# The first pair's up product made before the mix is known, and amended by a low-rank product

## The chip, the core and the metric

The kernel runs on one core of a Trainium2 chip. The metric is the device time of one execution in microseconds (us). Engines are named as in the profile: PE (TensorE matmul) with PEld (its weight loads), DVE (VectorE), ACT (ScalarE), POOL (GpSimd) and SP (SyncE, which here only issues DMAs).

## What is computed

Two stages follow each other: a gated linear recurrence with complex gates over 4 batches, 8 heads, 768 tokens and a head size of 48, and a mixer whose token mixing has rank 32.

```
# recurrence, per batch and head; S is 48 x 48
new_re = ar * S_re - ai * S_im
new_im = ar * S_im + ai * S_re
S_re, S_im = new_re + outer(k[t], v[t]), new_im
y[t] = q[t] @ S_re                       # gates a normalised to a magnitude of at most 0.999

# mixer, on x = y laid out as (batch, token, 8 * 48 = 384)
h  = x.transpose(0, 2, 1) @ U @ V        # U: 768 x 32, V: 32 x 768
u  = x + h.transpose(0, 2, 1)
ch = maximum(u @ w_ch1, 0) @ w_ch2       # w_ch1: 384 x 1536, w_ch2: 1536 x 384
out = u + ch
```

For one batch `u = x + V^T r` with `r = U^T x` (32 x 384). So `u @ w_ch1 = x @ w_ch1 + V^T (r @ w_ch1)`: the second term is a product of rank 32. The first needs only x of the tokens concerned, the second needs r, and so all 768 tokens of the batch.

## The kernel before, in words

Each batch's 768 tokens are six chunks of 128; there are 24 chunks, 0 to 23. For two chunks at a time (a group) `gates` computes magnitudes and angles, and for each chunk `prep` and `chain` do the recurrence in chunked form. A chunk's result x goes into one of eight buffers `xo` (line 873 copies it there from PSUM).

The mixer works on pairs of chunks; there are twelve pairs, three to a batch. `mixer(m)` for the first pair of a batch starts with `rank` (line 898): r as 24 matmul records over all six chunks, copied to SBUF at line 901. Every pair then has

- `spread` (line 914): V^T r for its two chunks,
- `mixed`: u = x + that (DVE, line 333), three transposes a chunk (line 927) and a copy into `uT` (line 929),
- `up` (line 939): six products, each of two 128-column blocks of w1 with the 256 columns of `uT` (12 records each, since an f32 matmul is recorded twice), followed by a Relu on ACT into `h`,
- the down product: for pair 0 `down` (line 1085), twice six pieces of h with w2; for later pairs `down_two` (line 1128), a form with fewer multiplications,
- `leave`: the result is sent out by POOL (line 1072).

The last six pairs use `up_fewer` (line 997) in place of `up`. `uT` and `h` have one buffer each, and the products `up` and `down` share two PSUM tiles (tag "M").

The weights come as 64-bit floats and are turned to f32 on the chip by `single`: twelve pieces of 768 KB and one for U and V, in the fixed order w1 (six), U and V, w2 (six). SP loads a piece into one of two staging slots (line 478), DVE converts it in six instructions (lines 487 to 497) into one of two further slots, and POOL adds it to its place by a DMA (line 500). The first half of w1's columns are pieces 0 to 2, the second half 3 to 5.

The order of all instructions is worked out on the host by `Plan`. Each piece of work is registered with an engine, a cost, a rank, and what it reads and writes. `Plan.order` lets every engine take the ready piece with the lowest rank (on SP and POOL too), and the kernel issues everything in this order. Ranks come from the table `URGENCY` by kind and number ("w1", "w2", "gates", "angles", "prep", "levels", "rest"; its values look like microseconds and are only compared with each other). Two kinds stand outside it: "small" comes before everything, "mixing" (the products `up` and `down`) after everything. So the mixing fills the gaps that the chunks leave. As long as no "mixing" work has begun, an idle PE is given spare products of the identity with itself (line 1252), whose result nobody reads.

Of the kernel before, what the change touches and what calls it, by code (L numbers as in the profile page):

```python
# [10 lines left out]
FP = mybir.dt.float32  # L11
# [12 lines left out]
BLK = 32  # L24

URGENCY = {
    "w1": {0: -1281.04, 1: -1220.88, 2: -1207.45, 3: 315.61, 4: 369.7, 5: 444.04, 6: 70.95},
    "w2": {0: -1266.56, 2: -21.8, 4: -981.82, 6: -74.99, 8: 354.48, 10: -1170.63, 12: 259.42},
    "gates": {0: 253.11, 1: -1390.93, 2: -0.7, 4: -1280.16, 6: 565.76, 8: -1068.17, 10: -187.84, 12: -54.04, 14: 550.2,
        16: 60.85, 18: -1317.29, 20: 219.78, 22: -1069.82},  # L30
    "angles": {0: -1303.82, 1: -1298.68, 2: -1227.51, 4: 58.46, 6: 57.41, 8: -1315.3, 10: -1053.02, 12: 620.73,
        14: 187.25, 16: -891.55, 18: 148.92, 20: -161.38, 22: -1298.55},
    "prep": {0: -1294.88, 1: 125.6, 2: -26.13, 3: 96.73, 4: 102.92, 5: 146.86, 6: 553.65, 7: 283.9, 8: 120.02,
        9: -991.17, 10: -32.91, 11: 113.94, 12: -202.96, 13: 14.8, 14: 318.58, 15: 357.43, 16: 269.94, 17: 521.08,
        18: 158.53, 19: -163.04, 20: 127.47, 21: 184.1, 22: 205.57, 23: -1204.94},
    "levels": {0: 201.22, 1: 294.56, 2: -15.94, 3: 207.38, 4: -1236.01, 5: 275.3, 6: 572.46, 7: 14.34, 8: -1057.92,
        9: 306.71, 10: 125.53, 11: 133.52, 12: 287.15, 13: 373.35, 14: 82.96, 15: 592.16, 16: 289.79,
        17: -1204.78, 18: -1075.08, 19: 91.86, 20: 733.17, 21: -1309.23, 22: 119.93, 23: -1230.17},
    "rest": {0: 93.55, 1: 47.27, 2: 273.41, 3: 257.67, 4: -1050.04, 5: -1068.08, 6: -1240.77, 7: -1208.87, 8: -1033.73,
        9: -1290.81, 10: 34.85, 11: -1143.56, 12: -162.29, 13: -197.24, 14: -1046.5, 15: 612.4, 16: 244.97,  # L40
        17: -1261.21, 18: 98.64, 19: -1031.75, 20: -1297.46, 21: 239.78, 22: 384.61, 23: 164.23},
}

# [144 lines left out]
def kernel(  # L189
# [76 lines left out]
    def buffer(base, tag, bufs, shape, space=None, padded=None):  # L266

        if tag not in pools:
            pools[tag] = pool(tag, bufs, **({"space": space} if space else {}))
        plan.buffer(base, tag, bufs, space is not None)  # L270
        kw = {"padded_shape": padded} if padded else {}
        makers[base] = lambda: pools[tag].tile(shape, FP, tag=tag, name=base[0], **kw)
# [7 lines left out]
    def get(*base):  # L280
        if base not in T:
            T[base] = makers[base]()
        return T[base]

    def psum(base, tag, shape, padded=None):
        buffer(base, "ps" + tag, 2, shape, PSUM, padded)

    def c_act(n):
        return 0.22 + 0.0008 * n  # L290

    def c_dve(n):
        return 0.15 + 0.00104 * n
# [8 lines left out]
    def PE(*a, **kw):  # L302
        plan.add("PE", *a, late=0.17, **kw)

    def ACT(cost, *a, **kw):
        plan.add("ACT", cost - 0.09, *a, late=0.09, **kw)

    def DVE(cost, *a, **kw):
        plan.add("DVE", cost - 0.09, *a, late=0.09, **kw)
# [22 lines left out]
    def add(o, a, b):  # L332
        nc.vector.tensor_tensor(out=o, in0=a, in1=b, op=OP.add)  # L333
# [60 lines left out]
    GATE = singles.tile([128, 6, GC * DM], FP, name="gate")  # L394
    AREA = {nm: GATE[:, n] for n, nm in enumerate(("x", "y", "n", "z", "ar", "ai"))}
    AREA.update({nm: AREA[nm].rearrange("p (c h d) -> p c h d", h=H, d=D) for nm in ("ar", "ai")})
    sums_w = singles.tile([128, 2, KF // 3 * 128], FP, name="sums")
    TS = []
    for n in range(3):
        TS.append(singles.tile([DQ, GC, H * NTOT], FP, name="T%d" % n))  # L400
# [475 lines left out]

    def mixer(m):
        i0 = m * MC  # L880
        b, c0 = where(i0)
# [4 lines left out]
        def out_of(nm, k, shape, padded):  # L886
            psum((nm, k), "M" if nm in ("up", "down") else "T", shape, padded)
            return nm, k

        if c0 == 0:  # L890
            buffer(r, "r", 1, [128, DM])
            ps = out_of("rank", b, [128, DM], [128, 512])

            def rank():
                for k in range(NCH // MC):
                    for n in range(NP):
                        c = n % MC * (NCH // MC) + k
                        nc.tensor.matmul(out=get(*ps)[n * R:(n + 1) * R], lhsT=U[:, c], rhs=get("xo", b * NCH + c), start=(k == 0),
                                         stop=(k == NCH // MC - 1), tile_position=(0, n * R))
            PE(2.0, R0, rank, [("UV", 0)] + [("xo", b * NCH + c) for c in range(NCH)], [ps], steps=2 * NP * NCH // MC)  # L900
            ACT(c_act(DM), R0, lambda: nc.scalar.copy(out=get(*r), in_=get(*ps)), [ps], [r])
        uT, h = ("uT", m), ("h", m)
        buffer(uT, "uT", 1, [128, KD, N])
        buffer(h, "h", 1, [128, KF, N])

        def spread():

            ps = [out_of("mixed", i0 + cc, [128, DM], [128, 512]) for cc in range(MC)]

            def products():  # L910
                for y in range(2):
                    for cc in range(MC):
                        at, c = slice(cc * MC * R, (cc + 1) * MC * R), c0 + cc
                        nc.tensor.matmul(out=get(*ps[cc])[:, y * DH:(y + 1) * DH], lhsT=V[at, c * CH:(c + 1) * CH],
                                         rhs=get(*r)[at, y * DH:(y + 1) * DH], start=True, stop=True, tile_position=(cc * MC * R, 0))
            PE(0.85, R0, products, [r, ("V", 0), uT + ("kept",)], ps, way=5, steps=8)
            return ps

        def mixed(cc, ps):
            i, c = i0 + cc, c0 + cc  # L920
            u = ("xo", i)
            DVE(c_dve(DM), R0, lambda: add(get(*u), get(*ps), get(*u)), [ps], [u])
            tr = out_of("uTp", i, [128, KD, CH], [128, 4, CH])

            def turn():
                for f in range(KD):
                    nc.tensor.transpose(out=get(*tr)[:, f], in_=get(*u)[:, f * 128:(f + 1) * 128], identity=ident)
            PE(0.35, R0, turn, [u], [tr], steps=KD)
            DVE(c_dve(DM), R0, lambda: nc.vector.tensor_copy(out=get(*uT)[:, :, cc * CH:(cc + 1) * CH], in_=get(*tr)), [tr],
                [uT + (cc,)])  # L930

        def up(ff):
            ps = out_of("up", (m, ff), [128, 2, N], None)
            lo = ff * 128 // WP * WP

            def products():
                for e in range(2):
                    for f in range(KD):
                        nc.tensor.matmul(out=get(*ps)[:, e], lhsT=w1[:, f, (ff + e) * 128:(ff + e + 1) * 128],  # L939
                                         rhs=get(*uT)[:, f], start=(f == 0), stop=(f == KD - 1))  # L940
            PE(2.6, RM, products, [uT] + [("w1", f, lo) for f in range(KD)], [ps], takes=[h], steps=4 * KD)
            ACT(c_act(2 * N), R0, lambda: act(get(*h)[:, ff:ff + 2], get(*ps), AF.Relu), [ps], [h + (ff,)])

# [135 lines left out]
        def down(cc):  # L1079
            i, c = i0 + cc, c0 + cc  # L1080
            ps = out_of("down", i, [128, DM], [128, 512])

            def products(f0):
                for ff in (f0, f0 + 1):
                    nc.tensor.matmul(out=get(*ps), lhsT=get(*h)[:, ff, cc * CH:(cc + 1) * CH], rhs=w2[:, ff],
                                     start=(ff == 0), stop=(ff == KF - 1))
            for f0 in range(0, KF, 2):
                PE(1.29, RM, lambda f0=f0: products(f0), [h + (f0,), ("w2", f0)], [ps], steps=4)
            o = ("xo", i)
            DVE(c_dve(DM), R0, lambda: add(get(*o), get(*ps), get(*o)), [ps], [o])  # L1090
            leave(cc)
# [78 lines left out]

        for cc, ps in enumerate(spread()):
            mixed(cc, ps)
        if m >= FEWER:
            up_fewer()
        else:
            for ff in range(0, KF, 2):
                up(ff)
# [24 lines left out]
    def chunks(g):  # L1202
        both = list(range(*GROUPS[g]))
        for these in [both] if g >= PAIRED else [[i] for i in both]:
            for i in these:
                load_qkv(i)
                prep(i)
            together([chain(i) for i in these])
            for i in these:
                if where(i)[1] == NCH - 1:  # L1210
                    for m in range(i // MC - NCH // MC + 1, i // MC + 1):
                        mixer(m)

    for n, nm in enumerate(AREA):
# [92 lines left out]
```

## Time and profile before

| | us |
|---|---|
| median of three runs (695.6 to 698.66) | 697.34 |
| the profiled execution | 698.57 |
| its span, first to last instruction | 696.8 |
| mean granted TensorE clock, share of full | 0.997 |
| first copy of chunk 1's x from PSUM | 83.5 |
| first rank product (batch 0 complete) | 133.1 |
| first up product of pair 0 / of pair 1 | 140.8 / 183.4 |
| rank products of batches 1, 2, 3 | 301.6, 454.7, 590.4 |

A profile's page gives busy time by engine and by groups of instructions; the stretches give the busy time of each engine between two moments; the views in order of time show single instructions. An engine that is busy need not be doing needed work: the spare products count as busy. A wait in the trace is named by the instruction that ended it.

### The profile page before, as it was taken

The page shows a single profiled execution, that of the slowest core. Times are in us where ns is not written, and L with a number is a line of the kernel's source. Part 1 is how long each engine was busy: PE and PEld are TensorE (multiplying, and loading weights), DVE is VectorE, ACT ScalarE, POOL GpSimd, SP SyncE. Part 2 cuts the span into 40 slices and gives each one's busy share as a digit, 9 for nine tenths or more (in the row PEclk, how much of TensorE's full clock was granted, in tenths as well). Part 3 has the DMA queues.
Part 4 walks back from the last instruction along what each step waited for, and adds up shares of the span by engine and source line. Part 5 has one row for each costly group of instructions (what it writes and reads, how often), then busy time and mean ns, then how long its engine had stood idle before and what let it go on. Part 6 is the DMA issues. An engine that isn't in the chain of part 4 may idle for free.

```text
span 696.8 us, 26972 instructions
## 1 busy us (share of the span) xinstructions
PE 673.7 (97%) x12116; PEld 594.2 (85%) x12116; DVE 538.9 (77%) x877; ACT 416.5 (60%) x776; POOL 51.8 (7%) x92
## 2 busy tenths in 40 slices
PE   8988998999999999999999999999998999999998
PEld 8777777786787888888888888889998898999998
DVE  5899999888998887758598668779886884555734
ACT  7879874968886897958796745434524325031230
POOL 5100000012100010001010100000000000000000
PEclk9999999999999999999999999999999999999999
DMA  8884745699514442432243031222111010000000
GB/s 202 190 187 86 172 99 105 171 222 189 110 36 97 87 92 54 94 70 57 51 89 78 3 86 40 45 43 56 37 36 18 14 41 2 18 7 24 7 18 24
DMA packets 165203, 53.24 MB, mean 76 GB/s; under 512 B 154016, under 2 KB 160352, under 8 KB 165088
## 3 DMA queue, kind: packets, MB, share of 16 engines
q1 hardware_dynamic: 161008, 42.26, 28.0%
q0 software_dynamic: 4080, 9.27, 5.9%
q8 instruction: 95, 1.56, 0.9%
q14 instruction: 20, 0.16, 0.1%
HBM read 33.59 MB, written 4.72 MB: 55 GB/s over the span
## 4 chain that ended last, share of the span: by engine, by line
PE 75%; ACT 10%; DVE 9%; issue 3%; DMA 2%; SPq 0%; DVEq 0%; ACTq 0%
PE down L1128 20%; PE few L997 12%; PE up L939 10%; PE tr L705 6%; PE inner L739 5%; ACT gate L327 4%; PE y L864 3%; PE dk L825 3%; DVE QK L330 2%; PE ks ps L810 2%; PE ph L650 2%; PE es ps L583 2%; PE tot L612 2%; PE y L856 2%; PE spare L1252 1%
## 5 line engine op out<-in xcount | busy, mean ns | idle before, releaser
L330 DVE TENSOR_TENSOR QK<-QK,T 112x1024 f32<-112x1024 f32 x120 | 145.4, 1217 | 7.6 <-PE corners L789 4.0
L939 PE MATMUL up<-uT,w 128*128 128x256 f32 x432 | 98.9, 382 | 0.0
L939 PEld LDWEIGHTS up<-uT,w 128*128 128x128 f32 x432 | 80.5, 190 | 12.3
L1005 ACT COPY h<-few 128x512 f32<-128x512 f32 x36 | 20.6, 586 | 95.0 <-PE few L997 78.2
L708 ACT COPY QK<-tr 112x512 f32<-112x512 f32 x96 | 53.0, 586 | 36.5 <-PE tr L705 36.1
L1128 PE MATMUL down<-w,h 128*128 128x192 f32 x396 | 74.1, 331 | 0.0
L327 ACT ACTIVATE gate<-gate 128x768 f32<-128x768 f32 (+1 forms) x91 | 70.2, 789 | 5.3 <-DMA gate<-in_a_re_dram 2.2
L1128 PEld LDWEIGHTS down<-w,h 128*128 128x128 f32 x396 | 63.7, 190 | 3.2 <-issue 1.1
L739 PEld LDWEIGHTS inner<-QK 112*32 112x32 f32 x4608 | 45.4, 109 | 20.7 <-issue 15.4
L333 DVE TENSOR_TENSOR h<-few,h 128x512 f32<-128x512 f32 x54 | 37.1, 690 | 31.3 <-PE few L997 28.7
L739 PE MATMUL inner<-QK 112*32 112x16 f32 (+1 forms) x4608 | 51.3, 190 | 10.4 <-issue 9.3
L1252 PE MATMUL spare<-ident 128*128 128x128 f32 x406 | 57.8, 289 | 1.7 <-POOL ident masks.py:199 1.5
L330 DVE TENSOR_TENSOR QKC<-qk,cs 128x768 f32<-128x768 f32 x48 | 45.7, 953 | 14.9 <-PE tr L705 13.4
L705 PE MATMUL tr<-ident,QKC 128*112 128x128 f32 x384 | 54.2, 276 | 2.8 <-ACT QK L708 1.1
L1252 PEld LDWEIGHTS spare<-ident 128*128 128x128 f32 x406 | 52.0, 200 | 5.5 <-POOL ident masks.py:199 1.5
L333 DVE TENSOR_TENSOR xo<-down,xo 128x192 f32<-128x192 f32 (+1 forms) x79 | 29.6, 385 | 28.5 <-PE down L1128 28.3
L705 PEld LDWEIGHTS tr<-ident,QKC 128*112 128x112 f32 x384 | 42.1, 133 | 10.9 <-ACT QK L708 3.0
L997 PE MATMUL few<-gate,w 128*128 128x128 f32 x336 | 44.0, 279 | 0.0
L1072 POOL DMA_DIRECT2D out_dram<-xo x32 | 18.8, 586 | 321.0 <-DVE xo L333 289.2
L873 ACT COPY xo<-y 64x192 f32<-64x192 f32 x96 | 30.0, 313 | 18.8 <-PE y L864 17.4
L997 PEld LDWEIGHTS few<-gate,w 128*128 128x128 f32 x336 | 40.6, 194 | 0.5
L1128 PE MATMUL down<-stage 128*128 128x192 f32 x198 | 36.8, 329 | 0.1
(131 smaller groups left out, 1242.6 us busy)
## 6 DMA issues: line engine op xcount, KB each, us to landing
stage<-in_moe_w_ch_dram SPq DMA_DIRECT2D x12, 768.0 KB, 5.8
gate<-in_a_re_dram SPq DMA_DIRECT2D x24, 192.0 KB, 3.5
gate<-in_a_im_dram SPq DMA_DIRECT2D x24, 192.0 KB, 3.7
qk<-in_q_dram SPq DMA_DIRECT2D x24, 192.0 KB, 3.4
qk<-in_k_dram SPq DMA_DIRECT2D x24, 192.0 KB, 4.2
VP<-in_v_dram SPq DMA_DIRECT2D x24, 192.0 KB, 3.4
T<-E SPq DMA_DIRECT2D x48, 96.0 KB, 2.7
w<-stage POOLq DMA_DIRECT2D x12, 384.0 KB, 6.0
```

The costliest lines, as they stand in the source:

```text
L327: return nc.scalar.activation(out=o, in_=i, func=f, **kw)
L330: nc.vector.tensor_tensor(out=o, in0=a, in1=b, op=OP.mult)
L333: nc.vector.tensor_tensor(out=o, in0=a, in1=b, op=OP.add)
L705: nc.tensor.transpose(out=get(*ps)[0:DQ, j], in_=get(*qkc)[:, hh * HH + j].rearrange("p u d -> p (u d)")[:, 0:DQ], identity=ident)
L708: ACT(c_act(HH * CH) - 0.05, R1, lambda u=u, hh=hh, ps=ps: nc.scalar.copy(out=get(*QK)[:, u, hh * HH:(hh + 1) * HH], in_=get(*ps)[0:DQ]), ...
L739: nc.tensor.matmul(out=get(*ps)[js, h], lhsT=k_of(h)[:, js], rhs=part(q_of(h)[:, js], "p"), start=True, stop=True, tile_position=(0, j * BLK))
L825: nc.tensor.matmul(out=get(*dk[r])[x:end, h], lhsT=get(*ks)[at, h, x:end], rhs=get(*VPi)[at, h], start=True, stop=True, tile_position=(r * ...
L873: ACT(c_act(HH * D), RR, lambda r=r, u=u: nc.scalar.copy(out=get(*xi).rearrange("p (a u d) -> p a u d", u=2, d=D)[r * HC:(r + 1) * HC, :, ...
L939: nc.tensor.matmul(out=get(*ps)[:, e], lhsT=w1[:, f, (ff + e) * 128:(ff + e + 1) * 128], rhs=get(*uT)[:, f], start=(f == 0), stop=(f == KD ...
L997: nc.tensor.matmul(out=get(*ps)[:, q], lhsT=w()[:, q * 128:(q + 1) * 128], rhs=v[0](), start=(n == 0 and q == 0), stop=True, skip_group_ch ...
L1128: nc.tensor.matmul(out=get(*to)[:, part], lhsT=x(j), rhs=y[:, j], start=(first and j == 0), stop=(j == KH - 1), skip_group_check=not first)
L1252: nc.tensor.matmul(out=spare[0], lhsT=ident, rhs=ident, start=True, stop=True)
```

## The change

For pair 0 alone, the up product is made as soon as chunks 0 and 1 are done, from x in place of u. Its two chunks are transposed into `uT`, and the six products are made in twelve pieces, all in one PSUM tile, each pair of which ACT copies to `h` without a Relu (`early`). When r is known, `amend` turns it, multiplies it by w1 (three blocks of four times 128 columns, lying below each other in one PSUM tile), and adds `(r w1)^T V` to `h` in three rounds; then a Relu is applied to `h` in place. Pair 0's `mixed` still makes u for the final sum, but has no transposes; pair 0's `down` waits for the whole of `h`. A small matrix `pick`, two identities of 32 below each other, sums the two partial results in which r lies. The table `URGENCY` is new throughout, and has a kind "early".

```diff
 URGENCY = {
-    "w1": {0: -1281.04, 1: -1220.88, 2: -1207.45, 3: 315.61, 4: 369.7, 5: 444.04, 6: 70.95},
-    "w2": {0: -1266.56, 2: -21.8, 4: -981.82, 6: -74.99, 8: 354.48, 10: -1170.63, 12: 259.42},
+    "w1": {0: -109.53, 1: -8.04, 2: 345.14, 3: 723.86, 4: 687.07, 5: 445.03, 6: 10.98},
+    "w2": {0: 76.19, 2: -211.9, 4: 131.04, 6: 421.14, 8: -515.83, 10: -186.39, 12: 1.07},
...
+    "early": {0: 98.86, 2: 63.89, 4: 678.21, 6: -80.97, 8: -124.56, 10: -198.18},
 }
...
+    pick = singles.tile([MC * R, R], FP, name="pick")
+    for n in range(MC):
+        nc.gpsimd.tensor_copy(out=pick[n * R:(n + 1) * R], in_=ident[n * R:(n + 1) * R, n * R:(n + 1) * R])
     sums_w = singles.tile([128, 2, KF // 3 * 128], FP, name="sums")
+    rT = sums_w[:, 0, 0:KD * R].rearrange("p (f r) -> p f r", r=R)
+    RW = sums_w[0:3 * R, 1]
...
+    def early():
...
+            PE(0.35, ("early", 0), turn, [("xo", cc)], [tr], steps=KD)
+            DVE(c_dve(DM), ("early", 0), lambda cc=cc, tr=tr: nc.vector.tensor_copy(
+                out=get(*uT)[:, :, cc * CH:(cc + 1) * CH], in_=get(*tr)), [tr], [uT + (cc,)])
...
+        for ff in range(0, KF, 2):
+            ps = ("up", (0, ff))
+            plan.buffer(ps, "first", 1, True)
+            makers[ps] = first
+            w = [("w1", f, ff * 128 // WP * WP) for f in range(KD)]
+            for e in range(2):
+                PE(1.3, ("early", ff), lambda ff=ff, e=e, ps=ps: product(ff + e, get(*ps)[:, e], get(*uT)), [uT] + w, [ps + (e,)],
+                   takes=[h], steps=2 * KD)
+            ACT(c_act(2 * MC * CH), ("early", ff), lambda ff=ff, ps=ps: nc.scalar.copy(out=get(*h)[:, ff:ff + 2], in_=get(*ps)), [ps],
+                [h + (ff,)])
+
+    def product(j, o, x):
+        for f in range(KD):
+            nc.tensor.matmul(out=o, lhsT=w1[:, f, j * 128:(j + 1) * 128], rhs=x[:, f], start=(f == 0), stop=(f == KD - 1))
+
+    def amend():
...
+        def turn():
+            for f in range(KD):
+                nc.tensor.matmul(out=get(*ps1)[:, f], lhsT=get(*r)[0:MC * R, f * 128:(f + 1) * 128], rhs=pick[0:MC * R], start=True,
+                                 stop=True, tile_position=(0, 0))
+        PE(0.3, R0, turn, [r], [ps1], way=5, steps=2 * KD)
+        DVE(c_dve(KD * R), R0, lambda: nc.vector.tensor_copy(out=rT, in_=get(*ps1)), [ps1], [to])
...
+        def weights():
+            for f in range(KD):
+                for g in range(NR):
+                    nc.tensor.matmul(out=get(*ps2)[g * R:(g + 1) * R], lhsT=rT[:, f], rhs=w1[:, f, g * n:(g + 1) * n], start=(f == 0),
+                                     stop=(f == KD - 1), tile_position=(0, g * R))
+        PE(2.7, R0, weights, [to] + [("w1", f, lo) for f in range(KD) for lo in (0, WP)], [ps2], way=6, steps=2 * KD * NR)
+        DVE(c_dve(n), R0, lambda: nc.vector.tensor_copy(out=RW, in_=get(*ps2)[0:NR * R]), [ps2], [to2])
+
+        for four in (((0, 1), (4, 5)), ((2, 3), (8, 9)), ((6, 7), (10, 11))):
...
+                        nc.tensor.matmul(out=get(*ps)[:, e], lhsT=RW[at, j * 128:(j + 1) * 128], rhs=V[at, 0:MC * CH], start=True,
+                                         stop=True, tile_position=(g * R, 0))
+            parts = [[h + (js[0],)] for js in four]
+            PE(1.0, ("mixing", 0), more, [to2, ("V", 0)] + parts[0] + parts[1], both, way=7, steps=8)
+            for js, ps, names in zip(four, both, parts):
+                o = lambda js=js: get(*h)[:, js[0]:js[1] + 1]
+                DVE(c_dve(2 * MC * CH), R0, lambda o=o, ps=ps: add(o(), get(*ps), o()), [ps], names)
+                ACT(c_act(2 * MC * CH), R0, lambda o=o: act(o(), o(), AF.Relu), [], names)
...
         uT, h = ("uT", m), ("h", m)
-        buffer(uT, "uT", 1, [128, KD, N])
-        buffer(h, "h", 1, [128, KF, N])
+        if m:
+            buffer(uT, "uT", 1, [128, KD, N])
+            buffer(h, "h", 1, [128, KF, N])
...
-            PE(0.85, R0, products, [r, ("V", 0), uT + ("kept",)], ps, way=5, steps=8)
+            PE(0.85, R0, products, [r, ("V", 0)] + ([uT + ("kept",)] if m else []), ps, way=5, steps=8)
...
             DVE(c_dve(DM), R0, lambda: add(get(*u), get(*ps), get(*u)), [ps], [u])
+            if not m:
+                return
...
-                PE(1.29, RM, lambda f0=f0: products(f0), [h + (f0,), ("w2", f0)], [ps], steps=4)
+                PE(1.29, RM, lambda f0=f0: products(f0), [h if m == 0 else h + (f0,), ("w2", f0)], [ps], steps=4)
...
-        if m >= FEWER:
+        if not m:
+            amend()
+        elif m >= FEWER:
             up_fewer()
...
                     for m in range(i // MC - NCH // MC + 1, i // MC + 1):
                         mixer(m)
+                elif i == MC - 1:
+                    early()
```

## The prediction

> **What bounds the kernel now.** I read the totals first, then the busy time of each engine by stage, then where the filler matmuls lie, then each engine in order of time around the join (the moment when all six chunks of the first batch are done and its rank product can run).
>
> ```profile
> PE 673.7 (97%) x12116; PEld 594.2 (85%) x12116; DVE 538.9 (77%) x877; ACT 416.5 (60%) x776; POOL 51.8 (7%) x92
> L939 PE MATMUL up<-uT,w 128*128 128x256 f32 x432 | 98.9, 382 | 0.0
> L1252 PE MATMUL spare<-ident 128*128 128x128 f32 x406 | 57.8, 289 | 1.7 <-POOL ident masks.py:199 1.5 <-issue 0.3
> w<-stage POOLq DMA_DIRECT2D x12, 384.0 KB, 6.0
> ```
>
> PE looks full, but 57.8 us of it is the spare product, which computes nothing. By stage, all engines (busy us; PE, PEld, DVE, ACT, POOL) and then the spare product alone:
>
> ```profile
> 84.00:121.00 37.00, 32.52 (x1030) 27.87 (x1029) 34.91 (x54) 21.89 (x45) 2.57 (x3) 1.00 0.52 104
> 121.00:133.10 12.10, 11.77 (x258) 9.35 (x257) 11.35 (x18) 10.99 (x26) 0.00 (x0) 1.00 0.65 176
> 140.80:158.40 17.60, 17.60 (x81) 14.95 (x80) 14.49 (x22) 11.62 (x19) 3.64 (x4) 1.00 0.85 196
> 158.40:301.60 143.20, 140.81 (x2788) 116.26 (x2787) 121.88 (x176) 119.68 (x214) 11.02 (x15) 1.00 0.46 96
> ```
>
> ```profile
> 84.00:121.00 37.00, 10.30 (x72) 1.00 0.52 104
> 121.00:133.10 12.10, 3.16 (x22) 1.00 0.65 176
> 133.10:140.80 7.70, 3.40 (x23) 1.00 0.76 186
> ```
>
> Before the join DVE is the full engine (94% in each of the first two stretches) and PE has room. From 140.8 on PE is full with real work: chunk products first, and the mixing of the finished batch in every gap. PE, SP and POOL in order of time around the join, then two pieces of the chain of waits that give clean PE paces:
>
> ```profile
> 133.13 2.44 PE L898 MATMUL mixed<-xo,UV 128*32 128x384 f32 x24
> 136.37 0.92 PE L914 MATMUL mixed<-r,V 64*128 64x192 f32 x8
> 140.81 7.94 PE L939 MATMUL up<-uT,w 128*128 128x256 f32 x36
> 149.22 7.93 PE L939 MATMUL up<-uT,w 128*128 128x256 f32 x36
> 178.92 4.04 PE L1085 MATMUL down<-w,h 128*128 128x384 f32 x12
> ```
>
> ```profile
> 119.60 1.47 SPq L478 DMA_DIRECT2D stage<-in_moe_w_ch_dram  x1
> 157.12 0.54 SPq L478 DMA_DIRECT2D stage<-in_moe_w_ch_dram  x1
> ```
>
> ```profile
> 114.91 0.86 POOL L500 DMA_DIRECT2D w<-stage  x1 [9.11 <-DVE stage L497]
> 172.12 0.90 POOL L500 DMA_DIRECT2D w<-stage  x1 [5.08 <-DVE stage L497]
> ```
>
> ```profile
> 252.55 2.59 PE up L939 x12
> 301.65 2.07 PE mixed L898 x24
> ```
>
> The up product of pair 0 is the 72 records from 140.8 to 157.0. The weights stand behind it: the six pieces of w2 are loaded from 119.6 to 157.1, one each 7.5 us, through two staging slots; the last is sent to its place at 172.1 and lands 6.0 us later, at 178.1. Pair 0's down product ends at 182.8, and only then is h free (it has one buffer), so that pair 1's up product, the next filler, can start. How much filler is left when the next rank product starts: after 301.65 five pieces of pair 2's down product still follow, some 4.9 us (0.98 each); after the third rank product at 454.7 ten (9.8 us), after the last at 590.4 fourteen (13.7 us).
>
> [...] here it was 0.997 over the span, and real products in the place of spare ones keep PE as busy, so I charge nothing for the clock.
>
> **The change part by part.** PE pace: 12 records of 256 columns in 2.59 us, 0.843 ns a column.
>
> Out of the full stage: the up product, 6 x 2.59 = 15.5 us, and its six transpose records (L927: 11.5 us for 72, so 1.0). Together 16.5 us.
>
> Into it: (a) r turned: 6 records of 32 columns, bounded by six weight loads of 186 ns below 1.1 us and by a spare-like 0.1 each above zero; 0.6. (b) r times w1: 18 records of 512 columns, three column groups abreast, so 6 x 512 = 3,072 columns; the rank product ran at 2.07 us for 6 x 384, 0.90 ns a column: 2.8 us (7.8 if they ran one after another). (c) the correction: 24 records of 256 columns, two abreast: 3,072 columns at 0.843 are 2.6, and three starts at the 0.2 us that L914's eight records took over their 4 x 192 columns: 3.3 (5.8 if not abreast). Sum 6.7 us. Net 9.8 us of PE less after the join.
>
> Into the front: 16.5 us of PE. Chunk 1's x is copied from PSUM by 84.8, so the room runs from about 84 to 133.1: spare 10.3 + 3.2, and PE idle 4.5 + 0.3, together 18.3 us. It fits, 90% full. The second half needs the last w1 piece (sent 114.9, landed 120.9): three pairs of 2.6 us with an ACT copy (0.59) and its handover, some 3.5 us each, are 10.5 us, in a stretch of 12.1. The price is blocking: an early piece is 1.3 us, two spare records are 0.22. A chunk's product that meets one waits half of it, 0.65 instead of 0.11; early pieces fill 15.5 of 49 us, and the chain has about 35 PE steps there: 35 x 0.32 x 0.54 = 6 us if nothing hides it, 0 where DVE sets the pace. DVE is 94% busy there; I take 2 us. DVE's two uT copies (0.55 each) move forward too, inside those 2 us. ACT gets six copies (3.5 us) in a front where it is 59% busy from 84 to 121: nothing. Two small POOL copies at the start lie ahead of the first sums, before 10.7; the first user on PE is at 16.8: nothing.
>
> After the join, on DVE: six adds of 512 columns (L333's h form, 0.69), rT (0.28) and RW (0.69): 5.1 us. They wait for PE, and behind them in DVE's queue stand w2 conversions and the next gates; DVE was 82% busy from 140.8 to 158.4, so I charge nothing by itself. The six Relus cost 0.63 instead of 0.60. No load is added; every load and its SP and POOL issue can move with the new table. The down product of pair 0 now waits for the whole h: r ready at 136.1, then 0.6 + 0.3 + 2.8 + 0.7 with handovers, three rounds of a 1.1 us product and two adds: about 15 us, so at 151, against 158.3 now.
>
> What is late next: w2. Nothing else can fill PE, because h has one buffer. So the 9.8 us don't come out by themselves; what counts is when pair 0's down product ends. Now it ends 4.7 us after the last landing, with 12 records still to do; with an earlier start only the last piece's two products of 1.29 remain, and 0.8 of handover: 3.4, a gain of 1.3 us. Staging itself can tighten: a slot needs 4.1 us of conversion (4 x 0.56 + 2 x 0.95), 0.9 to send, 6.0 to land: 11.0 for two slots, 5.5 a piece against 7.5, so up to 5 x 2.0 = 10 us. DVE, freed of a PE that it waited on, but with 5.1 us more to do, may give some of it; between 0 and 10 I take 4. The sum: -1.3 - 4 + 2 = -3.3 us. That is less than the 4.9 us of filler left at 301.65, so it carries to the end. The profiled execution was 698.57 us (span 696.8 and 1.8 around it) and becomes 695.3; the median, 1.2 lower at 697.34, becomes 694.0.
>
> **The rivals.**
> The full saving (B): the new order pulls the weights forward by some 12 us and all 9.8 us come out, less the 2 us of blocking: 689.5. For it: the whole table is new, and the staging floor allows 10. Against: 4.9 us of filler left at 301.65 caps the gain unless batch 1's chunks get done sooner as well (then 692.4).
> Weights late, slower (C): staging falls a period behind. Pieces pass the two slots strictly in order, w1, U and V, w2. The new table puts w1's pieces 3 to 5 at 724, 687 and 445 (before 316, 370, 444) and w2's at 76, -212, 131, 421, -516, -186 (before -1267, -22, -982, -75, 354, -1171), so DVE picks most of them later. Every us by which the last landing moves past 178.1 delays pair 1 and finds PE with nothing to do. One period, 7.5 us, less the 1.3: 703.5. It decides from a landing 1.3 us late, and can be measured from 4.8. Against it: DVE had gaps in this stage (3.1 us from 140.8 to 158.4) that take conversions whatever their rank.
> Not early after all: if the second half comes after the join, PE's saving shrinks by 7.8 us; it has the same cause as C and is counted there.
>
> **How the numbers follow.** The forecast (A) 0.42, its own range 690 to 697; B 0.18; C 0.36; others near no change or a little slower 0.04. A measurement of this kernel tells about 0.5%, 3.5 us, from no change. A gives 0.19 faster and 0.23 the same; B 0.17 faster, 0.01 the same; C 0.36 slower; the rest 0.02 and 0.02. So faster 0.36, same 0.26, slower 0.38. The range 685 to 706 leaves out B's lowest 0.03, C's upper 0.12 (two periods late, or blocking at its 6 us on top) and 0.02.
>
> **What would show it.** Spare falls from 57.8 to some 41 us, with L939-like products between 84 and the join; the rank product starts at 135 instead of 133; the correction takes 6 to 7 us of PE; PE shows idle time between the correction and the last w2 landing; pair 1's up product starts at about 179 instead of 183; the end moves by what that start moved. The forecast is wrong if the last w2 piece lands well before 172 or after 180, if the rank product slips by over 6 us, or if later stages, whose order the new table also changes, lose or gain more than this one.

## The result and the profile after

The changed kernel took 702.52 us (median of 16 runs, 697.79 to 707.86), the kernel before 697.31 (16 runs, 693.79 to 700.72): a ratio of 1.0069, 95% interval 1.0047 to 1.009. It is 0.7% slower, where a gain of 3.3 us had been forecast. Ratios and intervals here and below leave out runs over 1.5% above a kernel's fastest, which concerns four of experiment 10's 20 runs. The profiled execution of the changed kernel took 700.51 us, with a span of 698.7.

New line numbers: the rank product is L989, the early up product L921 into "first" (L921 into "up" is the later one), r's turn L933, r times w1 L945, the correction L961, the spare product L1348. Three lines from the page of the changed kernel:

```profile
PE 676.3 (97%) x12102; PEld 590.1 (84%) x12102; DVE 542.6 (78%) x885; ACT 418.6 (60%) x782; POOL 53.6 (8%) x94
L921 PE MATMUL up<-uT,w 128*128 128x256 f32 x360 | 82.2, 381 | 0.0
L1348 PE MATMUL spare<-ident 128*128 128x128 f32 x344 | 48.7, 290 | 1.5 <-POOL ident masks.py:199 1.5
```

Spare fell from 57.8 to 48.7 us; real PE work (PE less spare) rose from 615.9 to 627.6, by 11.7. The correction is 7.5 of that; the early pieces, each started by itself and one of them at a clock of 0.50, are busy for 19.3 us where the up product's two runs of 36 records took 15.9. Next PE in order of time (start, duration, then the line; a bracket is the idle time before it and what ended it):

```profile
114.05 0.38 PE L921 MATMUL first<-uT,w 128*128 128x256 f32 x1
116.23 2.50 PE L921 MATMUL first<-uT,w 128*128 128x256 f32 x5 [1.79 <-issue]
145.40 2.14 PE L989 MATMUL rank<-xo,UV 128*32 128x384 f32 x24
148.53 0.85 PE L933 MATMUL rTp<-pick,r 64*128 64x32 f32 x6
150.40 2.78 PE L945 MATMUL rwp<-w,sums 128*32 128x512 f32 x18
155.05 1.13 PE L961 MATMUL up<-V,sums 32*128 32x256 f32 x8
157.88 1.30 PE L961 MATMUL up<-V,sums 32*128 32x256 f32 x8
160.85 1.46 PE L961 MATMUL up<-V,sums 32*128 32x256 f32 x8
164.25 1.56 PE L1177 MATMUL down<-w,h 128*128 128x384 f32 x4
194.35 5.99 PE L921 MATMUL up<-uT,w 128*128 128x256 f32 x27
```

The join moved from 133.1 to 145.4, 12.3 us later. The landmarks, and the same counted from the join:

| | before, us | after, us | after less before | the same from the join |
|---|---|---|---|---|
| rank product of batch 0 | 133.1 | 145.4 | +12.3 | 0 |
| last w2 piece sent | 172.1 | 182.3 | +10.1 | -2.2 |
| pair 1's up product | 183.4 | 194.4 | +11.0 | -1.3 |
| rank product of batch 1 | 301.6 | 310.4 | +8.8 | -3.5 |
| rank product of batch 2 | 454.7 | 461.2 | +6.5 | -5.8 |
| rank product of batch 3 | 590.4 | 595.2 | +4.8 | -7.5 |
| end of the span | 696.8 | 698.7 | +1.9 | -10.4 |

So the saving after the join is there, 10.4 us by the end. The front gave back 12.3. The stretches of all engines in the changed kernel (from:to, length, busy us of PE, PEld, DVE, ACT and POOL, granted clock, DMA share, GB/s), and then the spare product alone in the first two:

```profile
84.00:121.00 37.00, 32.99 (x804) 26.32 (x803) 33.36 (x50) 26.04 (x50) 1.71 (x2) 0.95 0.53 114
121.00:133.10 12.10, 10.61 (x282) 8.74 (x279) 11.04 (x20) 3.88 (x11) 0.86 (x1) 1.00 0.63 119
```

```profile
84.00:121.00 37.00, 2.51 (x14) 1.90 (x14) 0.95 0.53 114
121.00:133.10 12.10, 0.00 (x0) 0.00 (x0) 1.00 0.63 119
```

Spare fell there from 13.5 to 2.5 us as planned, but PE still idles 5.5 us of the 49.1 (4.8 before) and the clock is no longer 1.00. The chain of waits from 84 us to the join, by line, first of before and then of after:

```profile
by line: ACT gate L327 12.0%; PE inner L739 9.7%; PE tr L705 8.9%; issue 8.0%; PE spare L1252 7.1%; DVE QK L330 7.1%; PE y L864 6.8%; PE dk L825 6.7%; ACT GL L327 3.4%; PE ph L653 3.4%; PE ph L650 3.2%; PE y L856 2.6%; ACT xo L873 2.5%; PE 
```

```profile
by line: PE first L921 22.8%; issue 11.4%; ACT gate L328 10.5%; PE dk L831 6.2%; PE spare L1348 5.8%; PE y L870 5.6%; PE inner L745 4.8%; PE tr L711 3.8%; PE ks ps L816 3.6%; ACT QK L714 3.2%; PE y L862 3.0%; ACT GL L328 2.6%; PE ph L656 2.
```

Of the 61.4 us, 22.8%, 14.0 us, are early products standing on the chain itself, and "issue" (PE waits for nothing that the profile shows) went from 8.0% of 49.1, 3.9 us, to 11.4%, 7.0 us. DVE, in all 6.7 us of the chain before (summed over its pieces in that view), has no piece on it after. The theories for the experiments follow from these rows: the early product is on the chain (work); DVE's extra conversion and the new order make the front late (order); stalls and a falling clock do (clock).

### The profile page after: what moved, and what is told of

It reads as the page before. It is cut to its first block, busy times and chain, and to the rows that moved or that the text cites. A ratio compares the mean times of both kernels' runs of the same rounds, so it can differ in the third digit from the quotient of the medians.

```text
span 698.7 us, 26957 instructions
## 1 busy us (share of the span) xinstructions
PE 676.3 (97%) x12102; PEld 590.1 (84%) x12102; DVE 542.6 (78%) x885; ACT 418.6 (60%) x782; POOL 53.6 (8%) x94
## 3 DMA queue, kind: packets, MB, share of 16 engines
q1 hardware_dynamic: 161008, 42.26, 27.8%
q8 instruction: 95, 1.56, 0.9%
## 4 chain that ended last, share of the span: by engine, by line
PE 74%; ACT 12%; DVE 10%; issue 3%; DMA 1%; DVEq 0%; ACTq 0%
PE down L1220 19%; PE few L1089 12%; PE up L921 8%; PE inner L745 5%; PE tr L711 4%; ACT gate L328 4%; PE dk L831 3%; PE y L870 3%; PE ks ps L816 2%; PE es ps L589 2%; PE first L921 2%; PE y L862 2%; PE ph L656 2%; PE tot L618 2%; PE spare L1348 2%
## 5 line engine op out<-in xcount | busy, mean ns | idle before, releaser
L921 PE MATMUL up<-uT,w 128*128 128x256 f32 x360 | 82.2, 381 | 0.0
L921 PEld LDWEIGHTS up<-uT,w 128*128 128x128 f32 x360 | 67.1, 190 | 9.8
L745 PEld LDWEIGHTS inner<-QK 112*32 112x32 f32 x4608 | 45.0, 110 | 16.2 <-issue 10.1
L1348 PE MATMUL spare<-ident 128*128 128x128 f32 x344 | 48.7, 290 | 1.5 <-POOL ident masks.py:199 1.5
L1348 PEld LDWEIGHTS spare<-ident 128*128 128x128 f32 x344 | 44.2, 202 | 4.3 <-POOL ident masks.py:199 1.5
L328 ACT ACTIVATE h<-h 128x512 f32<-128x512 f32 x42 | 26.2, 629 | 27.3 <-DVE h L334 27.2
```

The source lines that it names most:

```text
L328: return nc.scalar.activation(out=o, in_=i, func=f, **kw)
L745: nc.tensor.matmul(out=get(*ps)[js, h], lhsT=k_of(h)[:, js], rhs=part(q_of(h)[:, js], "p"), start=True, stop=True, tile_position=(0, j * BLK))
L921: nc.tensor.matmul(out=o, lhsT=w1[:, f, j * 128:(j + 1) * 128], rhs=x[:, f], start=(f == 0), stop=(f == KD - 1))
L1348: nc.tensor.matmul(out=spare[0], lhsT=ident, rhs=ident, start=True, stop=True)
```

## The experiments

**1 and 2. A third of the early product; long spare products in the old kernel.**

```
# 1, in the early product; two of the three blocks of the sum over x's 384 columns are left out
- for f in range(KD):  matmul(o, w1[:, f, j], x[:, f], ...)
+ for f in range(1):   matmul(o, w1[:, f, j], x[:, f], ...)
# 2, in the kernel before: 12 of the last 57 spare products, one in four
- matmul(spare, ident, ident)                      # 128 columns
+ for f in range(3): matmul(spare, ident, ident twice side by side)  # 256 columns, 1.3 us
```

> The changed kernel with its order kept, but each early product made of one matmul in place of three, so that 24 records instead of 72 run in the front, 10.3 us of PE less; the two thirds of x @ w1 that are left out are missing in pair 0's h. Theory P (PE's own time and its long pieces hold the chunks up): the first rank product comes at about 137 instead of 145.4, and the end some 8 us earlier. Theory O (the new order of the work on DVE and elsewhere makes the front long, whatever PE carries): the rank product stays at 143 to 146 and the end within 2 us of the changed kernel's.

> The kernel before with its order kept, but 12 of the 57 spare products that lie after 84 us are made as long as an early piece: three matmuls of 256 columns, 1.3 us in place of 0.22, some 13 us more on PE, as much as the change puts there. Nothing else differs. Theory P: the first rank product slips from 133.1 by 6 to 10 us, and the end by about as much. Theory O: it slips by under 3 us, because DVE sets the pace there and PE has 18 us of room.

Experiment 1: 705.39 us, ratio 1.0106 (1.0052 to 1.016). With 10.3 us less PE work the kernel was no faster, and the join came only 1.0 us sooner, at 144.4. The join is theory O's (143 to 146), the end is not: the median lies 2.9 us above the changed kernel's, not clear of noise by the two intervals. One line in order of time and two stretches of it say why neither theory is tested:

```profile
113.94 1.08 PE L831 MATMUL dk<-VP,ks 64*64 64x48 f32 x28 [4.27 <-issue]
```

```profile
110.00:115.00 5.00, 1.06 (x29) 0.97 (x29) 1.43 (x3) 1.61 (x3) 0.00 (x0) 0.68 0.73 204
115.00:120.00 5.00, 5.00 (x134) 3.55 (x137) 3.67 (x7) 1.95 (x4) 0.00 (x0) 0.64 0.07 12
```

PE stood 4.27 us with nothing to wait for in the profile, and ran the next 5 us at a clock of 0.64. The experiment had changed two things, and could not speak on the work.

Experiment 2: 709.04 us, ratio 1.0165 (1.0114 to 1.0216), clock 1.000 in every run. The spare products are now busy for 26.3 us between 84 and the join in place of 13.5. These 12.8 us more of PE work move the old kernel's join from 133.1 to 140.7 and its time by 11.5 us, although the kernel, its order, its weights and DVE's work are the old ones. The join is in theory P's range (6 to 10 us), the end slips by more than P said, and theory O (under 3 us) is out. PE now holds 55.8 of the 56.9 us of the chain from 84 to the join. The room of 18.3 us was not room. Four of the longest stretches of spare products in the old kernel between 84 and the join, in order of time:

```profile
90.57 2.17 PE L1252 MATMUL spare<-ident 128*128 128x128 f32 x18
108.40 1.16 PE L1252 MATMUL spare<-ident 128*128 128x128 f32 x8
115.46 1.83 PE L1252 MATMUL spare<-ident 128*128 128x128 f32 x14
120.74 1.05 PE L1252 MATMUL spare<-ident 128*128 128x128 f32 x7
```

Two of fifteen stretches are longer than one early piece of 1.3 us (the last one shown and its neighbour at 122.05, parted by 0.26 us, would together be a third); the others are 0.4 to 1.2 us. That this shortness is the reason is likely but not shown: no run splits the same work into shorter pieces.

**3 and 4. The stall: the first w2 piece's load later, alone and with a third of the product.** In the changed kernel SP sends U, V and the first w2 piece together at 105.6 to 106.6, and the DMA share is 0.99 from 112 to 114, just before PE's stall of 1.79 us.

```
+ order = plan.order()
+ load = <the SP load of the first w2 piece>
+ order: load moved behind the next six SP loads       # 3: alone; 4: with experiment 1's edit
```

> The changed kernel with one DMA moved in SP's queue: the 768 KB load of the first w2 piece, which is issued at 106.6 right behind U and V and not used before 123, goes behind the next six DMAs, to about 117. Nothing else differs. Theory F ([...] the wait of 1.8 us at 114.4 that nothing in the profile explains, and after it the clock of 0.50 from 116 to 119): the wait shrinks below 0.7 us, the clock stays at 1.0 there, the rank product comes 2 to 4 us earlier than at 145.4 and the end 2 to 3 us earlier. Rival (the wait and the clock are not that load's doing): wait and clock as before, rank product and end within 1 us.

> The same moved load together with the early products cut to one matmul of three (72 records become 24; two thirds of x @ w1 missing in pair 0's h), so that the cut is seen without the 4.3 us wait and the slow clock that covered it. Theory P (PE's time for the early products holds the chunks up): the rank product comes 4 to 8 us before that of the same kernel with whole products, about 136 to 140. Theory O (the order alone makes the front long): within 2 us of it.

Experiment 3: 700.65 us, ratio 1.0049 (1.0027 to 1.0071). Stretches of the changed kernel, then of experiment 3:

```profile
114.00:116.00 2.00, 0.43 (x3) 0.14 (x1) 2.00 (x4) 0.59 (x2) 0.00 (x0) 1.00 0.57 105
116.00:118.00 2.00, 1.77 (x4) 1.50 (x5) 1.31 (x3) 0.00 (x0) 0.00 (x0) 0.50 0.32 56
```

```profile
114.00:116.00 2.00, 2.00 (x72) 1.43 (x72) 1.83 (x4) 0.90 (x3) 0.00 (x0) 1.00 0.54 104
116.00:118.00 2.00, 2.00 (x12) 1.34 (x9) 2.00 (x4) 1.07 (x2) 0.00 (x0) 1.00 0.21 39
```

The stall and the clock of 0.50 are gone from this place, as theory F (both are this load's doing) said. But a clock of 0.50 came elsewhere, from 101.9 to 105.3 after a wait of 1.60 us, so that the mean clock from 84 to 121 stayed at 0.95, and the join came no sooner (146.3). The median is 1.9 us below the changed kernel's; the two intervals overlap, so this gain is not clear of noise.

Experiment 4 (which leaves out what experiment 1 does): 705.95 us, ratio 1.0122 (1.0087 to 1.0156), join at 147.3, within 2 us of experiment 3's, theory O's number. But the stall before the same products as in experiment 1 stayed, 2.35 us in place of 4.27, and the mean clock over its runs was 0.990. With the work taken away PE was busy for 37.2 of the 49.1 us from 84 to 133.1 (43.6 in the changed kernel), and the clock from 84 to 145.4 was 0.93 (0.97); the question of the work stayed open.

What PE waits for in these stalls can be read from the DMA and PE records of the traces. The changed kernel's page has a queue q8 named "instruction", with 95 packets and 1.56 MB. Its packets are 16 KB each, one for each 255 of PE's 24,204 records (matmuls and weight loads). The four waits of the changed front, 1.96, 1.79, 1.49 and 1.32 us long, each end 1.3 to 1.6 us after such a packet has landed. So do the five of the kernel before (0.26 to 1.10 us). From the first of the four waits to the others it is 760, 1,522 and 2,026 PE records, close to 3, 6 and 8 packets' worth; experiment 1's from 100 us on, 0.20, 4.27, 1.19 and 1.32 us, are 253, 253 and 381 matmuls and as many weight loads apart, close to 2, 2 and 3. From these counts I take it that PE was waiting for its own instructions; the profile names nothing that ended the waits. Why a packet comes late isn't shown: the four took 0.88 to 1.11 us themselves, where the median of all is 1.04. In all, such waits grew from 3.4 us in the front before to 6.6 after.

**5. What spare products are worth.**

```
# the kernel before: the last 57 spare products are not issued
- matmul(spare, ident, ident)
+ if len(calls) < 147: matmul(spare, ident, ident)
```

> The kernel before with its order kept, but the last 57 spare products (from 84 us on) left out; they compute nothing. Theory C ([...] the spare products pay): the granted clock falls under 0.99, products in the front show twice their time in places, and the end comes 2 to 6 us later. Rival (spare products only stand in the chunks' way there): the rank product comes 1 to 3 us earlier and so does the end.

702.72 us, ratio 1.0084 (1.005 to 1.0117). Its stretches:

```profile
84.00:121.00 37.00, 27.59 (x891) 22.67 (x892) 33.88 (x52) 20.60 (x43) 2.56 (x3) 0.83 0.51 101
121.00:133.00 12.00, 9.86 (x211) 7.73 (x207) 8.24 (x12) 9.51 (x19) 0.00 (x0) 0.64 0.62 171
```

Without its spare products the front runs at a clock of 0.83 and then 0.64, the join is 6.2 us later and the time 5.4 us longer, as theory C said. So spare products do real service here, and the forecast's "I charge nothing for the clock" was too quick.

**6 and 7. The order.** Each kernel with an order searched for it one instruction at a time, against the planner's own count of the time (a count made before launch, not a measurement: 699.1 to 696.2 for the changed kernel, 697.8 to 694.8 for the one before).

```
- for n in plan.order():
+ for n in ORDER:          # the searched list
```

> The changed kernel with another order and nothing else: each instruction group has its own rank in place of one from the table, searched on the host from the changed kernel's own order by the planner's count (699.1 us for the changed kernel's table, 696.2 for this order; the kernel before's table counts 697.8). Theory T (the new table was not searched well enough, and the structure itself gains): this order is clearly faster than the kernel before, 693 us or less. Theory S (the saved products are given back by the structure, since the correction, the staging of w2 and the longer front cost as much as they bring): it gains the 3 us of the count over the changed kernel and lands at 698 to 700, not below the kernel before by more than 1 us.

> The control: the kernel before with an order searched in the same way, for about as many steps, from its own order (planner's count 694.8 in place of 697.8). Theory S: it gains about 3 us too, to some 694 to 695, and stays 2 to 5 us ahead of the changed kernel with its searched order. Theory T: it gains less than the changed structure, and comes out no faster than that one.

Experiment 6: 702.81 us, ratio 1.0098 (1.0063 to 1.0133), join at 148.2, with a stall of 4.6 us (the profiled execution is the slowest of its six, 706.78). Experiment 7: 699.59 us, ratio 1.0037 (1.0013 to 1.0061), join at 132.3. Neither count came true, nor a theory's time: both searched orders were to gain 3 us, and neither did. Of theory S only the distance came in, 3.2 us between the two kernels (2 to 5). But as the planner's count misled for both, this search says little of what a better order could bring, and the share of the new order in the slip stays open.

**8 and 9. Double the early product; half of it behind the join.** Experiment 2, with 12.8 us more work in the front, had a clock of 1.000 in every run; experiments 1 and 4, with less, had 0.987 to 0.995. So more work should keep the clock out of the answer.

```
# 8: each early piece issued twice, the second over the first
- lambda: product(ff + e, ...)
+ lambda: [product(ff + e, ...) for _ in range(2)]
# 9: pairs 10, 8, 6 of the early product moved behind rank, rTp and rwp
+ for ff, after in ((10, "rank"), (8, "rTp"), (6, "rwp")):
+     <the three instructions of ("early", ff) moved behind that PE step>
```

> The changed kernel with each early product issued twice, the second time over the first: 15.5 us more of PE work before the join, nothing else, and the order kept. P (early PE work lies on the front's path at the rate of the change, 12.3 us of slip for 16.5 us of work, 0.75): the rank product moves from 145.4 to about 157 (152 to 160), and the time to about 712 (708 to 718). O (the slip comes from the new order itself, its conversions and DVE's picks, and PE still has room): the rank product stays under 149 and the time under 706. [...]

> The changed kernel with the second half of the early product (pairs 10, 8 and 6, six of its twelve pieces, 7.8 us, with their copies) moved behind the rank product, in the gaps of the correction's first steps. P (linear, 0.75 us of slip per us of early work): the rank product comes at about 139.5 (138 to 141.5), join to end grows by up to 7.8 us from 553.3, and the time stays where the changed kernel's is, 700 to 703. R (the front has room for half the product, the slip belongs to the second half): the rank product at 136.5 or earlier, and the time 696 to 699. O (the slip is the order's, not the work's): the rank product stays at 143 or later and the time goes to 706 or more.

Experiment 8: 712.69 us, ratio 1.0226 (1.0186 to 1.0265), clock 0.997 to 1.000. The join is at 153.5, 8.1 us later for 15.5 us of added work, and the time 10.2 us longer than the changed kernel's: in theory P's ranges, out of theory O's. Its chain of waits from 84 to 154:

```profile
by line: PE first L921 45.6%; PE inner L745 8.7%; PE ks ps L816 5.3%; issue 4.2%; PE y L870 4.1%; PE tr L711 3.3%; PE spare L1348 3.1%; PE dk L831 3.1%; PE y L862 2.8%; PE es ps L589 2.1%; PE ph L656 1.9%; PE ph L659 1.8%; ACT L325 1.8%; AC
```

45.6% of 70 us are 32 us: practically the whole doubled product (12 x 2.7) stands on the chain. At the join that is 0.52 us per us, close to experiment 2's 7.6 for 12.8 (0.59). It is a net rate: "issue" on the chain fell from 7.0 to 2.9 us here.

Experiment 9: 718.4 us, ratio 1.032 (1.028 to 1.036), the join at 148.3. The numbers are the order theory's, but the run doesn't show its cause, since the clock fell:

```profile
121.00:133.00 12.00, 9.23 (x266) 7.88 (x266) 9.73 (x18) 2.60 (x8) 0.37 (x1) 0.50 0.56 109
146.00:160.00 14.00, 12.35 (x71) 9.09 (x70) 5.72 (x10) 3.68 (x6) 1.62 (x2) 0.87 0.57 128
```

With half the pieces gone from the front it ran at a clock of 0.50 for 12 us, and after the join the moved pieces stand in front of the correction, while DVE is busy 5.72 and ACT 3.68 of 14 us. As a test of the work it is blurred in the way of experiments 1 and 4.

**10 and 11. Shorter pieces, the same number of instructions.**

```
# two of each piece's three matmuls over 16 columns instead of 256; 11: with experiment 3's move too
- matmul(out=o, lhsT=w1[:, f, j], rhs=x[:, f], ...)
+ matmul(out=o[:, :n if f else None], lhsT=w1[:, f, j], rhs=x[:, f, :n if f else None], ...)   # n = 16
```

> The changed kernel with its order and its number of instructions, but of each early product's three matmuls the second and third run over 16 columns instead of 256, so a piece should take some 0.7 us instead of 1.3: about 7 us less PE work before the join and the same count of instructions to fetch. The output leaves out most of two thirds of pair 0's x times w1. W (the slip is the early work itself, at the 0.5 to 0.75 us per us that doubling it and the change show): the rank product moves from 145.4 to 140 to 142, and the time to 696 to 699. K (work taken out of the front only leaves PE idle, and its clock falls): the clock over 100 to 133 drops below 0.9, the rank product stays at 143.5 or later, and the time is 701 or more.

> The same shortened early products, with the first w2 piece's load behind the next six loads, which took away the 1.8 us stall of the changed kernel before. W: no stall over 1 us near 113, clock 1.0 over 108 to 121, the rank product at 139 to 142 and the time 694 to 698. K: a stall of over 1 us appears elsewhere in 100 to 133 with the clock below 0.9 over it, the rank product at 143.5 or later and the time 700 or more.

A piece went from 1.46 us to 0.95, so 6.1 us less work. Experiment 10: 702.01 us, ratio 1.0037 (1.0014 to 1.0061). Experiment 11: 703.16, ratio 1.0092 (1.0057 to 1.0127), join at 147.0, clock 0.78 from 121 to 133. Experiment 10's stretches:

```profile
110.00:121.00 11.00, 9.10 (x281) 7.53 (x280) 9.69 (x14) 6.42 (x15) 0.00 (x0) 0.82 0.61 151
121.00:133.00 12.00, 12.00 (x249) 11.22 (x248) 8.40 (x15) 3.55 (x9) 0.00 (x0) 0.50 0.51 101
```

In the profiled executions the clock theory's numbers came in (0.82 and 0.50, join at 145.9). But experiment 10's runs differ in clock, and so in time, and that helps to tell the two causes apart. Runs at a mean clock of 1.000:

| | runs at clock 1.000 | their median, us | median of all runs |
|---|---|---|---|
| before | 29 of 86 | 695.9 | 697.6 |
| changed | 2 of 16 | 699.6 | 702.5 |
| 3, load moved | 4 of 14 | 698.0 | 700.7 |
| 8, early product doubled | 2 of 4 | 712.2 | 712.7 |
| 10, pieces shortened | 1 of 20 | 695.1 | 702.0 |
| 2, before with long spares | 4 of 4 | 709.0 | 709.0 |

(The 86 are all runs of the kernel before beside the experiments.) At full clock the time grows with the work in the front, but the rates differ: 6.1 us less early work in experiment 10 is worth 4.5 us (699.6 to 695.1, two runs against one), or 0.74 us per us; straight lines of time against clock through all runs of both kernels give 3.2 us at full clock, 0.52. The 15.5 us more of experiment 8 cost 12.6 (0.81), and the 12.8 us more of experiment 2 cost 13.1 (1.02). These are rates of the whole time and hold effects after the join too, so they can't be set against the 10.4 us saved there. At full clock the changed kernel is 3.7 us slower. The rest of the 4.9 us between the medians of the table, 1.2, is clock: the changed kernel's runs have a mean of 0.9961, those of before 0.9978, and their medians lie 2.9 and 1.7 us above their own full-clock values.

## Why the prediction was wrong

**The front, the step that failed.** "The price is blocking: … 6 us if nothing hides it, 0 where DVE sets the pace … I take 2 us." Measured: 12.3 us, against 10.4 saved behind the join. Both ends were too low, for two reasons. First, "room" was counted as a sum (18.3 us of spare and idle PE); experiment 2 shows that 12.8 us put into it are not free, and that its stretches are mostly shorter than a piece (two of fifteen are longer) is the likely reason. Second, DVE's 94% was read as "DVE sets the pace". The chain of waits of before already said otherwise: of its 49.1 us PE holds 27.8, ACT 10.9 and DVE 6.7. A full engine beside a chain isn't the chain. The forecast's half-a-piece estimate, 0.65 us a meeting, supposes that pieces meet the chain at random; in fact nine of the twelve early pieces stood on it whole, 14.0 us of them in the profiled front.

How the 12.3 us divide is not fully shown. PE's waits for instructions, as I read them, which the forecast didn't have, hold 3.1 us more of the chain than before ("issue", 3.9 to 7.0). The 3.4 us at a clock of 0.50 can cost up to half their length, 1.7 us, by my estimate. That leaves some 7.5, about the 7.6 that experiment 2's 12.8 us of work cost in the old order; but this is an estimate from these rows, and what the new order itself brings wasn't separated.

**The clock.** "Real products in the place of spare ones keep PE as busy." PE's busy sum did stay (43.6 against 44.3 us of 49.1), but longer waits replaced short ones (1.3 to 2.0 us in place of 0.3 to 1.1). After the one of 1.79 us the granted clock was 0.50 from 116.0 to 119.4; in the 3.4 us before that spell, as long as the spell itself, PE had been busy for 1.65. This term, charged at nothing, is about 1.2 us of the difference between the medians (2.9 less 1.7).

**The full stage.** Net 9.8 us less PE after the join was forecast. The correction's parts took 0.85, 2.78 and 1.13 + 1.30 + 1.46, so 7.5 us against 6.7: the turn and the correction's rounds were dearer than their terms, r times w1 as computed. Both products ran abreast as priced (2.78 us against 7.8 and 3.9 against 5.8 for one after another). The span from the join to the end fell by 10.4: PE's busy time in it by 7.9 (553.6 to 545.7), less than the net 9.8, and its idle time by 2.5. The forecast let only 5.3 of it come out (3.3 and the 2 of blocking); here it was too cautious. Nearly half of the 10.4 (4.6) comes after batch 2's rank product. Whether the smaller PE load or the new order of the later stages brings that late part wasn't separated; doubling the early product lengthened this span to 559.3, so it also feels the front.

**w2.** "What is late next: w2" came true, and the tighter staging did not. The first piece of w2 before, then the first and the last after:

```profile
134.30 0.86 POOL L500 DMA_DIRECT2D w<-stage  x1 [18.54 <-DVE stage L497]
```

```profile
136.25 0.86 POOL L506 DMA_DIRECT2D w<-stage  x1 [4.45 <-DVE stage L503]
182.26 0.86 POOL L506 DMA_DIRECT2D w<-stage  x1 [6.69 <-DVE stage L503]
```

The first piece was 2.0 us later than before, the last 10.1. The five steps between them took 46.0 us in place of 37.8, so 9.2 a piece in place of 7.6: staging fell about one period behind, as rival C said. The late front doesn't explain that. In experiment 2, with the front 7.6 us late in the old order, the five steps took 38.6 us; in experiments 3 and 8, with the new table, 46.3 and 46.2. The forecast's own sign, "after 180", called it wrong, and pair 1's up product started at 194.4 instead of 179 (counted from the join 1.3 us sooner, where 1.3 plus 4 had been forecast). C's price, a PE with nothing to do, isn't seen: from 164.2 to 194.4 PE was busy 28.96 of 30.2 us, with chunks. What the slower staging costs was not tested by a run of its own. C's number, 703.5, lies close to the measured 702.5, but it has no slip of the front by 12.3 us in it, so that closeness is in part luck.

**The signs.** Spare 48.7 instead of 41 (2.7 us of it run between 133.1 and the later join, another 2.8 between the correction's steps); rank product at 145.4 instead of 135, past the 6 us that were named as the limit; correction 7.5, just over "6 to 7". A small misreading: by its own line pair 0's up product before ended at 157.2, not 157.0; nothing rests on it.

No version here beats the kernel before. The best complete version of the changed kernel is experiment 3, 0.5% slower than before.

## What to carry to other kernels

The sum of idle and filler time on an engine is not yet room; read the lengths of the gaps and the chain of waits before moving work into a stage that hands over between engines. Set what is saved behind the join against the rate at which the front pays for it: here the join moved by 0.5 to 0.6 us per us of added work, and the correction takes 7.5 of the 16.5 us first. Don't put a stretch's lateness down to the stage before it without reading its first step as well as its last. On PE, compare runs at the same granted clock before explaining a few us, since leaving PE's products out can cost more than it gives (in experiment 5, 57 spare products: 5.4 us, with the clock at 0.83 and 0.64).

## What the hardware showed unexpectedly

- Less work, slower: dropping 57 spare products (experiment 5) cost 5.4 us; cutting 10.3 us of matmuls (experiment 1) made the changed kernel no faster.
- The granted clock fell to 0.50 in spells: 3.4 us in the changed kernel (116.0 to 119.4) and in the one before (525.5 to 528.9), 17.1 us in experiment 10. In six profiled executions (before, changed, experiments 1, 3, 5 and 10), in the 3.4 us before each of the eight spells looked at, PE had been busy for 1.05 to 1.85 us. None of these stretches was idle as a whole.
- The clock of 0.50 in experiment 10 lasted from 117.1 to 134.2, and through 12 us (121 to 133) in which PE is shown as busy 12.00 of 12.00, though that busy time is partly modelled. What ended it isn't shown.
- PE stood up to 4.6 us (experiment 6) where it waited for nothing that the profile shows. In the front of the kernel before and of the changed one, such waits ("issue") end 1.3 to 1.6 us after a 16 KB packet of the queue "instruction" has landed. Moving one load took the one of 1.79 us that ended at 116.2 away (experiment 3); others appeared elsewhere (1.60 us, ended at 100.7, for one). What delays a packet is open.
- One kernel's runs spread by their clock: over the 86 runs of before, a straight line gives 7.6 us for each 0.01 of mean clock.
